# Gateloop and low-rank mixer: 96 packed rows, group 0's logarithms summed in the product, the sign from bits, and another written-out order

## The chip, the cores and the metric

The kernel runs on 1 core of one Trainium2 chip. The metric is the device time of one execution in microseconds; lower is better. A core has five engines that run side by side, each through its own list of instructions in order: TensorE (PE, with its weight loads PEld), VectorE (DVE), ScalarE (ACT), GpSimd (POOL) and SyncE (SP, which here only issues transfers). Semaphores tie them together.

## The reference, cut to what matters

```python
mag = np.sqrt(a_re * a_re + a_im * a_im)
scale = np.minimum(mag, 0.999) / (mag + 1e-06)
a_re_n, a_im_n = (a_re * scale, a_im * scale)
for t in range(S):
    ar, ai = (a_re_n[:, :, t, :, None], a_im_n[:, :, t, :, None])
    new_re = ar * S_re - ai * S_im
    new_im = ar * S_im + ai * S_re
    S_re, S_im = (new_re + kv, new_im)       # kv = outer(k_t, v_t)
    y[:, :, t] = q_t @ S_re
...
h = xt @ U @ V                               # xt: y's heads side by side, turned
u = x + h.transpose(0, 2, 1)
return u + np.maximum(u @ w_ch1, 0.0) @ w_ch2
```

Four batches, eight heads of 48, sequences of 768. The first half is a recurrence with a complex decay for each channel; the second mixes tokens with a product of rank 32 and channels with a layer of width 1536. All is in float32.

## The kernel before, in words

**Chunks and groups.** The recurrence is done in 24 chunks of 128 tokens, six to a batch, two to a group: groups 0 to 11. A decay is split into the logarithm of its magnitude and its angle, both are summed over tokens, and exponentials and sines of the sums weigh q and k, so that the recurrence becomes products of matrices. Then a mixer follows for every two chunks: 12 mixers.

**Gates of a group** (`gates`, `magnitudes_of` from line 637). DVE and ACT form the logarithm `l` of the magnitude and the tangent of half the angle. For group 0 (`SPREAD`) the work is split by chunk, and `l` is made of two parts: DVE takes the maximum (line 658) and adds `y` to it (line 660). PE sums `l` over tokens with one matmul for `es ps` and one for `ef ps` (line 696), and block totals `tot` (line 735). From group 3 on (`SPLIT`) `l` is split in two words first (lines 670 to 673), line 692 sums them and line 741 makes the totals. The sign of the real part comes from its bits on DVE in groups 0 to 2 (`BITS`, line 678), and from ACT's Sign in the others (line 681). There ACT also turns the angle into fractions of a turn and adds a quarter (line 763), after DVE's product in line 760. ACT loads another table between the exponentials and the sines (line 381).

**Preparation of a chunk** (`prep`). DVE weighs q and k by `es`, multiplies them with cosine and sine (`cs`) into `QKC`, and PE transposes `QKC` head by head (line 860), in two halves of 64 tokens side by side. A head's `QKC` has the real part in columns 0 to 47 and the imaginary part in 64 to 111, with zeros between, so transposed rows are 112 (`DQ`); the tables `T` of block decays have the same rows, with ones in between from POOL (line 469), and come from `E` by four transfers of SP (line 719). ACT copies the transposed halves to `QK` (line 871).

**A chunk's products** (`chain`). `inner` (lines 907, 910), `corners` (971), the state products `dk` (996) and the output `y` (1027, 1035), with scalings of `QK` on DVE between them and four transfers of SP that place diagonal blocks (`AT`).

**Mixers** (`mixer`). `rank` (1070), ACT's copy of it to `r` (1076), `mixed` (1089), then `up` (1122) and `down` (1313, 1356), or `few` (1222) in late mixers. Mixer 0 starts early, before its low-rank part is known, and is put right: `rT` (1136) transposes `r`, DVE copies it, `rw ps` (1145) multiplies it with the weights, ACT copies that, and `fix` (1161) is added to `h`. The weights come as float64 and are turned to float32 by DVE and ACT (line 384 for ACT, 573 to 580 for DVE).

**The order** is written out by hand. Every operation of every engine has a place in one long list; the table `ORDER` gives, for each engine and kind of work, the places of its operations. The instructions are issued in the order of places, so each engine's list is in that order; a place says nothing of a time. `SPARE` gives, for some places, how many units of filler PE issues ahead of the operation there: `idle` (line 1519) multiplies the identity with one to three copies of itself, 128 columns a unit, into a PSUM tile that the next product overwrites. A float32 matmul runs as two passes and is counted twice in the profile; a transposition is counted once. So the order fixes what each engine has to do ahead of any given operation. Ahead of ACT's copy of `r` stand 210 ACT operations, and ahead of `rT` 111 PE operations besides fillers; ahead of the first transposition of chunk 7 stand 271 ACT and 228 DVE operations.

Of the kernel before, what the change touches and what calls it, by code (L numbers as in the profile page):

```python
# [10 lines left out]
FP = mybir.dt.float32  # L11
# [28 lines left out]
        ("POOL", "load"): {0: [14], 1: [34], 1.5: [84], 2: [31]},  # L40
        ("DVE", "load"): {1: [58]},
# [6 lines left out]
        ("ACT", "gates"): {0: [1, 2, 4, 6, 7, 16, 17, 22, 23, 29, 28, 45, 70, 71], 1: [24, 27, 38, 39, 41, 42, 46, 47, 65, 64, 67, 68], 2: [129, 108,  # L48
# [10 lines left out]
        ("DVE", "gates"): {0: [5, 8, 13, 18, 19, 54, 49], 1: [30, 21, 40, 43, 44, 51, 50], 2: [111, 143, 156, 185, 169], 4: [277, 322, 323, 372, 356],  # L59
# [10 lines left out]
        ("ACT", "angles"): {0: [72, 86, 98, 100, 103], 1: [76, 106, 112, 114, 126], 2: [210, 231, 251, 240, 241, 242, 263, 269, 271], 4: [375, 395,  # L70
# [5 lines left out]
        ("DVE", "angles"): {0: [81, 89], 1: [87, 107], 2: [211, 232, 252], 4: [376, 402, 425], 6: [589, 597, 602, 612, 625, 626, 665], 8: [698, 716,  # L76
# [4 lines left out]
        ("DVE", "prep"): {0: [85, 104, 110], 1: [121, 128, 145], 2: [226, 250, 265], 3: [203, 304, 309], 4: [373, 424, 427], 5: [443, 470, 472], 6:  # L81
# [159 lines left out]
def kernel(  # L241
# [19 lines left out]

    nc = tc.nc
    B, H, S, D = q.shape
    DP = 64
    DQ = DP + D
    DM = H * D  # L270
    FF = moe_w_ch1.shape[1]
    R = moe_U.shape[1]
    KD = DM // 128
# [1315 lines left out]
```

## Time and profile before

| what | value |
|---|---|
| median of 3 runs | 629.38 us (629.16 to 630.21) |
| span of the profiled execution, first to last instruction | 627.0 us |
| PE busy | 609.9 us, of which fillers (line 1519) 30.6 us |
| DVE busy | 499.7 us |
| ACT busy | 415.8 us |
| transfers | 45.7 MB, mean 73 GB/s |

The median lies 2.4 us above the profiled span; no other time is given for the profiled execution itself. In the profile's lines an instruction group reads as line, engine, operation, result<-inputs, shape and count, then busy time and the mean of one in ns, then the idle time of its engine in front of it with what ended that. A line of a window reads as stretch, length, then busy time and count for each engine, the granted clock of TensorE, the share of time in which the DMA engines were busy, and GB/s. A line of the timeline starts with the start and the length in microseconds; there, "x6" are six instructions in a row.

### The profile page before, as it was taken

To read this page: it belongs to the slowest core of one execution; us is meant where nothing else is said; L and a number is where in the kernel's file an instruction comes from. 1 tells how busy PE (TensorE), PEld (TensorE's weight loads), DVE (VectorE), ACT (ScalarE), POOL (GpSimd) and SP (SyncE) were. 2 spreads that over 40 slices of the span, in tenths; PEclk is the share of its full clock that TensorE was granted. 3 is DMA by queue.
4 is the path that set the end of the run, shared out by engine and by line. 5 is a ranking of instruction groups with operands and counts; after the bars stand their busy time and mean duration, and the time that the engine had idled before them with its cause. 6 is when DMAs were issued, how large, how long until landed. Compare 5 with 4: busy or idle time off the path is not lost.

```text
span 627.0 us, 23447 instructions
## 1 busy us (share of the span) xinstructions
PE 609.9 (97%) x10380; PEld 526.2 (84%) x10380; DVE 499.7 (80%) x887; ACT 415.8 (66%) x807; POOL 38.1 (6%) x79
## 2 busy tenths in 40 slices
PE   6998989999999999999999999999999999999998
PEld 3566767666889889889989989888999998999997
DVE  6899999888999979758977867788989884464554
ACT  6999999999898988687787867688433431202010
POOL 5000000000001010010000100000100100000100
PEclk7999999999999999999999999999999999999999
DMA  8864565644143252541512512601203020000101
GB/s 211 191 146 115 135 136 132 155 111 104 33 80 76 50 120 44 99 89 28 99 37 46 113 40 46 124 19 25 63 21 60 9 51 3 1 1 1 45 14 44
DMA packets 173685, 45.74 MB, mean 73 GB/s; under 512 B 167632, under 2 KB 170384, under 8 KB 173584
## 3 DMA queue, kind: packets, MB, share of 16 engines
q1 hardware_dynamic: 171376, 39.90, 30.1%
q0 software_dynamic: 2208, 4.35, 2.1%
q8 instruction: 81, 1.33, 0.9%
q14 instruction: 20, 0.16, 0.1%
HBM read 33.59 MB, written 4.72 MB: 61 GB/s over the span
## 4 chain that ended last, share of the span: by engine, by line
PE 77%; ACT 4%; DVE 3%; DMA 1%; issue 1%; SPq 0%; ACTq 0%; DVEq 0%
PE down L1356 24%; PE up L1122 15%; PE few L1222 11%; PE dk L996 3%; PE tr L860 3%; PE y L1035 3%; PE inner L910 2%; PE down L1313 2%; PE inner L907 2%; PE tot L741 2%; PE y L1027 2%; PE mixed L1089 2%; PE es ps L692 1%; PE ef ps L692 1%; PE uTp L1107 1%; PE corners L971 1%
## 5 line engine op out<-in xcount | busy, mean ns | idle before, releaser
L1122 PE MATMUL up<-uT,w 128*128 128x256 f32 x504 | 116.9, 383 | 0.0
L387 DVE TENSOR_TENSOR QK<-QK,T 112x512 f32<-112x512 f32 (+2 forms) x144 | 102.1, 732 | 8.4 <-PE inner L910 4.3
L1122 PEld LDWEIGHTS up<-uT,w 128*128 128x128 f32 x504 | 93.6, 190 | 12.5
L1356 PE MATMUL down<-w,h 128*128 128x192 f32 x396 | 72.2, 331 | 0.0
L384 ACT ACTIVATE gate<-gate 128x768 f32<-128x768 f32 (+1 forms) x82 | 64.8, 795 | 7.4 <-DVE GS L791 3.2
L1356 PEld LDWEIGHTS down<-w,h 128*128 128x128 f32 x396 | 64.1, 190 | 1.5 <-issue 0.7
L871 ACT COPY QK<-tr 112x512 f32<-112x512 f32 x96 | 51.2, 590 | 14.6 <-PE tr L860 14.3
L390 DVE TENSOR_TENSOR xo<-down,xo 128x192 f32<-128x192 f32 (+1 forms) x79 | 29.9, 387 | 27.5 <-PE down L1356 27.0
L387 DVE TENSOR_TENSOR QKC<-qk,cs 128x768 f32<-128x768 f32 x44 | 41.7, 955 | 6.3 <-ACT cs L384 3.6
L1230 ACT COPY h<-few 128x512 f32<-128x512 f32 x30 | 17.2, 586 | 40.8 <-PE few L1222 40.8
L1356 PE MATMUL down<-stage 128*128 128x192 f32 x198 | 37.6, 331 | 0.0
L1111 ACT COPY uT<-uTp 128x384 f32<-128x384 f32 x22 | 10.0, 479 | 41.4 <-PE uTp L1107 26.9
L1222 PE MATMUL few<-gate,w 128*128 128x128 f32 x280 | 34.8, 275 | 0.0
L1298 POOL DMA_DIRECT2D out_dram<-xo x32 | 19.2, 644 | 243.3 <-DVE xo L390 140.0
L860 PEld LDWEIGHTS tr<-ident,QKC 64*112 64x112 f32 x768 | 24.5, 130 | 10.7 <-issue 4.7
L1222 PEld LDWEIGHTS few<-gate,w 128*128 128x128 f32 x280 | 33.3, 192 | 0.0
L1356 PEld LDWEIGHTS down<-stage 128*128 128x128 f32 x198 | 32.1, 190 | 0.7 <-issue 0.2
L779 POOL DMA_DIRECT2D gate<-F x15 | 12.0, 799 | 327.9 <-DVE w L578 113.5
L860 PE MATMUL tr<-ident,QKC 64*112 64x64 f32 x768 | 29.4, 221 | 2.3 <-DVE QKC L387 1.6
L381 ACT ACT_TABLE_LOAD x24 | 30.8, 1283 | 1.1 <-PEq L1573 0.7
L384 ACT ACTIVATE h<-up 128x512 f32<-128x512 f32 x42 | 24.6, 596 | 9.8 <-PE up L1122 9.5
L976 ACT COPY AT<-corners 32x128 f32<-32x128 f32 x96 | 24.2, 255 | 9.6 <-PE corners L971 8.3
(200 smaller groups left out, 1285.4 us busy)
## 6 DMA issues: line engine op xcount, KB each, us to landing
stage<-in_moe_w_ch_dram SPq DMA_DIRECT2D x12, 768.0 KB, 5.0
qk<-in_q_dram SPq DMA_DIRECT2D x24, 192.0 KB, 3.2
qk<-in_k_dram SPq DMA_DIRECT2D x24, 192.0 KB, 2.7
VP<-in_v_dram SPq DMA_DIRECT2D x24, 192.0 KB, 3.6
gate<-in_a_re_dram SPq DMA_DIRECT2D x22, 192.0 KB, 3.4
gate<-in_a_im_dram SPq DMA_DIRECT2D x22, 192.0 KB, 3.4
AT<-DG SPq DMA_DIRECT2D x96, 32.0 KB, 2.3
T<-E SPq DMA_DIRECT2D x48, 48.0 KB, 2.9
```

Of the source, the lines that this page charges most:

```text
L381: ACT(1.37, rank, lambda: nc.scalar.preload_act_table_set(name), writes=[TABLE])
L384: return nc.scalar.activation(out=o, in_=i, func=f, **kw)
L387: nc.vector.tensor_tensor(out=o, in0=a, in1=b, op=OP.mult)
L390: nc.vector.tensor_tensor(out=o, in0=a, in1=b, op=OP.add)
L860: nc.tensor.transpose(out=get(*ps[r])[0:DQ, h], in_=get(*qkc)[at, h].rearrange("p u d -> p (u d)")[:, 0:DQ], identity=ident[at, at], tile_ ...
L871: nc.scalar.copy(out=to, in_=a)
L976: ACT(0.36, RR, lambda r=r, u=u: nc.scalar.copy(out=get(*ATi).rearrange("p (a u) t -> p a u t", u=2)[r:r + BLK, :, u, BLK:2 * BLK], in_=ge ...
L996: nc.tensor.matmul(out=get(*dk[r])[x:end, h], lhsT=get(*ks)[at, h, x // DP, 0:end - x], rhs=get(*VPi)[at, h], start=True, stop=True, tile_ ...
L1122: nc.tensor.matmul(out=get(*ps)[:, e], lhsT=w1[:, f, (ff + e) * 128:(ff + e + 1) * 128], rhs=get(*uT)[:, f], start=(f == 0), stop=(f == KD ...
L1222: nc.tensor.matmul(out=get(*ps)[:, q], lhsT=w()[:, q * 128:(q + 1) * 128], rhs=v[0](), start=(n == 0 and q == 0), stop=True, skip_group_ch ...
L1298: queue.dma_start(out=out[b, c * CH:(c + 1) * CH, lo:hi], in_=get("xo", i)[:, lo:hi])
L1356: nc.tensor.matmul(out=get(*to)[:, part], lhsT=x(j), rhs=y[:, j], start=(first and j == 0), stop=(j == KH - 1), skip_group_check=not first)
```

## The change

1. **96 rows.** `DQ` is 96: a head's real and imaginary part stand side by side in `QKC`, `T` and `QK`, without columns between. POOL's memsets of `T` go, and those of `QKC` shrink to 16 columns at the end. The state products still take 64 and 48 columns of a head's `QKC`; the last 16 of these belong to the next head and their sums are not read.
2. **Group 0's logarithms** are no longer added on DVE. PE sums both parts: two products where there was one in `es ps`, `ef ps` and each block total of chunks 0 and 1.
3. **The sign from bits** in all groups, on DVE. ACT's Sign and its Identity in groups 3 to 11 go; the quarter is added by the operations that split the angle in two words.
4. **Another order.** All of `ORDER` and `SPARE` is new, from a search in which every transfer took a microsecond longer. The units of filler are 108 instead of 153: 39 ahead of the first `es ps` (before: 8), none behind place 606, which is `rT` (before: the last at 718; `rT` had 596). Ahead of ACT's copy of `r` stand 213 ACT operations, ahead of `rT` 112 PE operations besides fillers, and ahead of the first transposition of chunk 7 260 ACT and 221 DVE operations.

```diff
-SPARE = {20: 8, 32: 9, 62: 1, 66: 1, 73: 1, 82: 5, 91: 1, 113: 6, 116: 1, 119: 8, 140: 8, 153: 6, 157: 4, 167: 1, 168: 1, 207: 6, 216: 1, 217: 1, 282:
-         1, 352: 2, 436: 1, 514: 5, 518: 5, 527: 4, 546: 4, 547: 25, 551: 12, 596: 2, 601: 1, 606: 3, 624: 1, 632: 3, 646: 1, 653: 1, 664: 1, 672: 2,
-         678: 5, 694: 1, 695: 1, 717: 1, 718: 2}
+SPARE = {20: 39, 82: 6, 94: 2, 106: 10, 119: 5, 140: 9, 155: 3, 157: 2, 191: 6, 227: 6, 257: 6, 263: 2, 277: 3, 311: 3, 336: 2, 439: 2, 606: 2}
...
+    DQ = 2 * D
     DP = 64
-    DQ = DP + D
...
+    SUMMED = (0,)
...
-        QKC.append(singles.tile([128, H, 2, DP], FP, name="QKC%d" % n))
-        nc.gpsimd.memset(QKC[n][:, :, :, D:DP], 0.0)
+        QKC.append(singles.tile([128, H * DQ + DP - (DQ - DP)], FP, name="QKC%d" % n))
+        nc.gpsimd.memset(QKC[n][:, H * DQ:], 0.0)
...
         TS.append(singles.tile([DQ, GC, H * NTOT], FP, name="T%d" % n))
-        nc.gpsimd.memset(TS[n], 1.0)
...
-            if on_dve:
+            if g in SUMMED or g in SPREAD:
                 DVE(c_one(W), R1, lambda: nc.vector.tensor_scalar(out=t(l), in0=t(l), scalar1=-0.5, scalar2=-LNMAX, op0=OP.mult,
                                                                   op1=OP.max), [], [L])
-                DVE(cd, R1, lambda: add(t(l), t(l), t(y)), Y, [L])
+                if g not in SUMMED:
+                    DVE(cd, R1, lambda: add(t(l), t(l), t(y)), Y, [L])
...
-            if g in BITS:
-                DVE(c_one(W), R1, lambda: nc.vector.tensor_scalar(out=t(n).bitcast(U32), in0=t(ar).bitcast(U32), scalar1=0x80000000,
-                                                                  scalar2=INV_PI, op0=OP.bitwise_and, op1=OP.bitwise_or), AR, [N])
-            else:
-                ACT(ca + 0.09, R1, lambda: act(t(n), t(ar), AF.Sign, bias=tiny), AR, [N])
+            DVE(c_one(W), R1, lambda: nc.vector.tensor_scalar(out=t(n).bitcast(U32), in0=t(ar).bitcast(U32), scalar1=0x80000000,
+                                                              scalar2=INV_PI, op0=OP.bitwise_and, op1=OP.bitwise_or), AR, [N])
...
-                    PE(0.65, R1, lambda: nc.tensor.matmul(out=get(*to), lhsT=m.bitcast(FP), rhs=of(l, i), start=True, stop=True),
-                       [L, name], [to, ("sums", g, i)], takes=[keeps], steps=2)
+                    def each():
+                        for u, a in enumerate(parts):
+                            nc.tensor.matmul(out=get(*to), lhsT=m.bitcast(FP), rhs=of(a, i), start=(u == 0), stop=(u == len(parts) - 1))
+                    PE(0.65 * len(parts), R1, each, [L, name] + [y + (i,)] * (g in SUMMED), [to, ("sums", g, i)], takes=[keeps], steps=2 * len(parts))
...
-                        out=get(*tt)[u * DP:u * DP + D, 0:hi - lo, w * HH * NTOT:(w + 1) * HH * NTOT],
+                        out=get(*tt)[u * D:(u + 1) * D, 0:hi - lo, w * HH * NTOT:(w + 1) * HH * NTOT],
...
-            if g not in BITS:
-                ACT(ca + 0.09, R2, lambda: act(t(z), t(z), AF.Identity, scale=1.0 / math.pi, bias=fourth), [], Z)
...
-                    ACT(c_act(DM), R2, lambda: nc.scalar.copy(out=of(a, i), in_=of(z, i)), [zi], [a + (i,)])
+                    ACT(c_act(DM) + 0.09, R2, lambda: act(of(a, i), of(z, i), AF.Identity, bias=fourth), [zi], [a + (i,)])
...
-                        nc.tensor.transpose(out=get(*ps[r])[0:DQ, h], in_=get(*qkc)[at, h].rearrange("p u d -> p (u d)")[:, 0:DQ],
+                        nc.tensor.transpose(out=get(*ps[r])[0:DQ, h], in_=get(*qkc)[at, h * DQ:(h + 1) * DQ],
...
-                    for x, end in ((0, DP), (DP, DQ)):
-                        nc.tensor.matmul(out=get(*dk[r])[x:end, h], lhsT=get(*ks)[at, h, x // DP, 0:end - x], rhs=get(*VPi)[at, h],
+                    for x, w in ((0, DP), (DP, D)):
+                        nc.tensor.matmul(out=get(*dk[r])[x:x + w, h], lhsT=get(*ks)[at, h * DQ + x:h * DQ + x + w], rhs=get(*VPi)[at, h],
```

In the order's first places, for instance, the transfers are issued otherwise (the numbers are places; kinds 0 to 0.1 are group 0's real and imaginary parts and the prefix matrix, 1 and 2 the first two blocks of weights, 1.2 the masks, 1.3 and 1.4 chunk 0's q, k and v):

```diff
-        ("SP", "load"): {0.0: [0, 3, 2666, 2654, 2670], 0.05: [11, 12], 0.1: [9], 1: [10], 1.2: [57], 1.3: [15, 59], 1.4: [83], 2: [35], 2.5: [56,
+        ('SP', 'load'): {0.0: [0, 4, 2655, 2640, 2658], 0.05: [11, 7], 0.1: [9], 1: [22], 1.2: [21], 1.3: [55, 73], 1.4: [91], 2: [23], 2.5: [79, 83],
```

More of the change, by code (lines that the diff above doesn't have):

```diff
@@ L76 @@
-        ("DVE", "angles"): {0: [81, 89], 1: [87, 107], 2: [211, 232, 252], 4: [376, 402, 425], 6: [589, 597, 602, 612, 625, 626, 665], 8: [698, 716,
[4 rows of a table removed]
-        ("DVE", "prep"): {0: [85, 104, 110], 1: [121, 128, 145], 2: [226, 250, 265], 3: [203, 304, 309], 4: [373, 424, 427], 5: [443, 470, 472], 6:
[6 rows of a table removed]
-        ("ACT", "prep"): {0: [115, 117, 120, 122], 1: [158, 147, 154, 160], 2: [266, 270, 283, 281], 3: [319, 320, 327, 318], 4: [442, 439, 446, 445],
[4 rows of a table removed]
-        ("DVE", "rest"): {0: [118, 149, 155, 175, 159, 170, 194], 1: [174, 229, 234, 259, 209, 235, 248, 253], 2: [288, 315, 325, 366, 291, 314, 324,
[8 rows of a table removed]
@@ L102 @@
-        ("DVE", "levels"): {0: [123, 135, 148, 136, 137, 152], 1: [177, 192, 202, 195, 198, 225], 2: [292, 302, 308, 301, 303, 312], 3: [328, 371,
[9 rows of a table removed]
-        ("ACT", "levels"): {0: [138], 1: [215], 2: [305], 3: [378], 4: [468], 5: [530], 6: [766], 7: [839], 8: [947], 9: [1006], 10: [1152], 11:
[14 rows of a table removed]
-        ("ACT", "rest"): {0: [191, 182, 200, 201, 219, 223, 222], 1: [255, 261, 256, 258, 280, 279, 278], 2: [342, 341, 336, 335, 385, 390, 391], 3:
[10 rows of a table removed]
-        ("ACT", "small"): {0: [595, 285, 307, 492, 396, 554, 590, 549, 623, 636], 1: [744, 791, 777, 807, 782, 856, 859], 2: [984, 978, 1088, 1139,
[4 rows of a table removed]
@@ L172 @@
-        22: [2039, 2077]},
-        ("DVE", "mixing"): {7: [2018, 2019, 2021, 2030, 2032, 2024, 2040, 2102, 2108, 2115, 2120, 2125, 2027]},
-}
-SPARE = {20: 8, 32: 9, 62: 1, 66: 1, 73: 1, 82: 5, 91: 1, 113: 6, 116: 1, 119: 8, 140: 8, 153: 6, 157: 4, 167: 1, 168: 1, 207: 6, 216: 1, 217: 1, 282:
-         1, 352: 2, 436: 1, 514: 5, 518: 5, 527: 4, 546: 4, 547: 25, 551: 12, 596: 2, 601: 1, 606: 3, 624: 1, 632: 3, 646: 1, 653: 1, 664: 1, 672: 2,
-         678: 5, 694: 1, 695: 1, 717: 1, 718: 2}
[9 rows of a table added]
+        ('POOL', 'load'): {0: [10], 1: [62], 1.5: [578], 2: [42]},
@@ new lines @@
+        ('DVE', 'load'): {1: [26]},
[6 rows of a table added]
+        ('ACT', 'gates'): {0: [2, 3, 5, 13, 17, 14, 19, 46, 47, 33, 34, 44, 69, 70], 1: [15, 8, 25, 29, 28, 32, 40, 57, 52, 49, 59, 65], 2: [121, 61,
[10 rows of a table added]
+        ('DVE', 'gates'): {0: [6, 1, 27, 18, 63, 56], 1: [16, 12, 30, 31, 67, 39], 2: [90, 145, 153, 196, 148], 4: [221, 306, 319, 353, 327], 6: [441,
[10 rows of a table added]
+        ('ACT', 'angles'): {0: [71, 85, 93, 92, 99], 1: [81, 97, 102, 108, 114], 2: [211, 235, 249, 248, 246, 250, 255, 254, 269], 4: [364, 390, 411,
[5 rows of a table added]
+        ('DVE', 'angles'): {0: [76, 86], 1: [84, 98], 2: [214, 236, 253], 4: [371, 391, 416], 6: [554, 557, 563, 591, 611, 612, 624], 8: [699, 727,
[4 rows of a table added]
@@ new lines @@
+        ('DVE', 'prep'): {0: [88, 103, 107], 1: [110, 118, 131], 2: [208, 256, 262], 3: [239, 287, 309], 4: [398, 419, 424], 5: [429, 442, 490], 6:
[6 rows of a table added]
+        ('ACT', 'prep'): {0: [111, 115, 117, 116], 1: [127, 130, 156, 159], 2: [264, 270, 271, 272], 3: [316, 308, 335, 323], 4: [448, 444, 436, 437],
[4 rows of a table added]
+        ('DVE', 'rest'): {0: [113, 146, 158, 201, 144, 154, 167], 1: [198, 205, 222, 252, 228, 260, 265, 268], 2: [280, 321, 334, 351, 298, 333, 348,
[8 rows of a table added]
+        ('DVE', 'levels'): {0: [124, 135, 139, 133, 137, 147], 1: [160, 179, 195, 178, 186, 210], 2: [275, 289, 291, 290, 293, 312], 3: [350, 370,
[9 rows of a table added]
@@ new lines @@
+        ('ACT', 'levels'): {0: [138], 1: [189], 2: [303], 3: [386], 4: [488], 5: [541], 6: [743], 7: [839], 8: [933], 9: [1033], 10: [1170], 11:
[14 rows of a table added]
+        ('ACT', 'rest'): {0: [183, 204, 176, 200, 219, 225, 231], 1: [238, 258, 241, 243, 285, 286, 282], 2: [366, 384, 363, 376, 407, 405, 410], 3:
[10 rows of a table added]
+        ('ACT', 'small'): {0: [605, 296, 415, 467, 385, 526, 596, 610, 619, 622], 1: [733, 802, 778, 770, 812, 835, 749], 2: [919, 916, 1060, 1082,
[4 rows of a table added]
+        ('DVE', 'small'): {0: [278, 608, 627, 631, 637, 634, 671, 653, 645, 650, 750, 720], 1: [713, 719, 712, 825, 819, 842, 896, 921, 873, 901, 915,
[25 rows of a table added]
@@ new lines @@
+        ('POOL', 'small'): {0: [996, 823], 1: [1053, 1096, 1110], 2: [1389, 1184, 1397], 3: [1668, 1429, 1495], 4: [1716, 1633, 1738], 5: [2067, 1867,
+        1944], 6: [2229, 2076, 2183], 7: [2315, 2247, 2301], 8: [2639, 2477, 2533], 9: [2631, 2522, 2659], 10: [2610, 2600, 2625]},
+        ('POOL', 'angles'): {6: [598], 8: [725, 740], 10: [879, 906], 12: [1067], 14: [1255, 1292], 16: [1418, 1477], 18: [1648], 20: [1807, 1864],
+        22: [1994, 2031]},
+        ('DVE', 'mixing'): {7: [1995, 2009, 1996, 2047, 2060, 1983, 1985, 2091, 2106, 2116, 2108, 2115, 2095]},
+}
@@ L301 @@
     PL = H * HC
-    BITS = range(SPLIT[0])
     PUT = (0, 2), (4, 6), (8, 10)
@@ L443, in w2_of @@
         return w2.rearrange("p (j x) m -> p j x m", x=2)[:, :, x, y * DH:(y + 1) * DH]
-    leps, lmax, tiny = column("leps", math.log(1e-6)), column("lmax", LNMAX), column("tiny", 1e-30)
+    leps, lmax = column("leps", math.log(1e-6)), column("lmax", LNMAX)
     magic, fourth, quarter = column("magic", MAGIC), column("fourth", 0.25), column("quarter", math.pi / 2)
@@ L726, in of_blocks @@
             lo = first
-            ps, e = ("tot", i), ("E", g)
+            ps, e, parts = ("tot", i), ("E", g), (y, l) if g in SUMMED else (l,)
             psum(ps, "T", [128, HH, NTOT])
@@ L734, in sums @@
                         h, w = at + (u * HH + p) * D, 64 if u == 0 else D
-                        nc.tensor.matmul(out=get(*ps)[u * 64:u * 64 + w, p], lhsT=get(*l)[:, h:h + w], rhs=total, start=True,
-                                         stop=True, tile_position=(0, u * 64))
+                        for n, a in enumerate(parts):
+                            nc.tensor.matmul(out=get(*ps)[u * 64:u * 64 + w, p], lhsT=get(*a)[:, h:h + w], rhs=total, start=(n == 0),
+                                             stop=(n == len(parts) - 1), tile_position=(0, u * 64))
             def at_once():
@@ L744, in of_blocks @@
             else:
-                PE(0.51, R1, sums, [l, ("total", 0), ("sums", g)], [ps], way=1, takes=[e], steps=4 * HH)
+                PE(0.2 + 0.31 * len(parts), R1, sums, [l, ("total", 0), ("sums", g)] + [y + (i,)] * (g in SUMMED), [ps], way=1, takes=[e],
+                   steps=4 * HH * len(parts))
             used = 2 * D if g in SPLIT else 64 + D
@@ L833, in T_of, with turns_of_heads @@
         return get("T", g)[:, i - GROUPS[g][0]].rearrange("p (h b) -> p h b", h=H)[:, :, at:]
+    def turns_of_heads(qkc):
+        return get(*qkc)[:, 0:H * DQ].rearrange("p (h u d) -> p h u d", u=2, d=D)
     def prep(i):
@@ L988, in chain @@
         for r in parts_k:
-            psum(dk[r], "Y", [128, H, D], [128, H, DP])
+            psum(dk[r], "Y", [128, H, D], [128, H, HC])
         def state(h0):
```

24 lines of the change are left out of this document (8 added, 16 removed), and 246 rows, old and new, of the table ORDER.

## The prediction

> **What bounds the kernel now.** I read the page first, for the shares of the span, then busy time by stage, then the timeline at the stage's border, then the groups for single prices.
>
> ```profile
> span 627.0 us, 23447 instructions
> PE 609.9 (97%) x10380; PEld 526.2 (84%) x10380; DVE 499.7 (80%) x887; ACT 415.8 (66%) x807; POOL 38.1 (6%) x79
> PE   6998989999999999999999999999999999999998
> DVE  6899999888999979758977867788989884464554
> ACT  6999999999898988687787867688433431202010
> ```
>
> PE has 97% of the span, but not all of that is work: line 1519 issues filler matmuls whose result nobody reads. The next two answers split the span at two landmarks, the first `rT` matmul (line 1136, at 119.3 us) and the first transposition of chunk 7 (line 860, at 163.0 us): first all instructions, then the fillers alone.
>
> ```profile
> 0.00:119.30 119.30, 106.66 (x2222) 76.23 (x2222) 110.58 (x189) 109.06 (x212) 8.41 (x32) 0.97 0.64 153
> 119.30:163.00 43.70, 42.66 (x424) 28.18 (x424) 38.46 (x57) 39.23 (x61) 2.50 (x3) 1.00 0.41 98
> 163.00:627.00 464.00, 460.58 (x7744) 421.76 (x7734) 350.66 (x644) 267.54 (x536) 27.16 (x44) 1.00 0.24 50
> ...
> 0.00:119.30 119.30, 24.59 (x70) 14.10 (x70) 0.97 0.64 153
> 119.30:163.00 43.70, 6.01 (x22) 3.60 (x22) 1.00 0.41 98
> 163.00:627.00 464.00, 0.00 (x0) 0.00 (x0) 1.00 0.24 50
> ```
>
> The columns after the length are busy time and count of PE, PEld, DVE, ACT and POOL (in the filler rows PE and PEld alone), then clock, DMA share and GB/s. In the first stage PE's useful time is 106.66 − 24.59 = 82.1 us of 119.3, while DVE and ACT are busy for 110.6 and 109.1: these two set the pace. In the second, PE's useful time is 42.66 − 6.01 = 36.65, below ACT's 39.23 and DVE's 38.46: they still set it, just. From 163 us on there is no filler and PE idles 3.4 us, nearly all of it the tail behind the last matmul: from here the time is PE's work.
>
> So time can be won in three ways: reaching 119.3 sooner, having nothing to fill between the landmarks, or less PE work afterwards.
>
> **The change part by part.** *Up to the landmark `rT`.* It waits for ACT's copy of `r` (line 1076), and ACT works in the order written down.
>
> ```profile
> 118.34 0.70 PE L1519 MATMUL fix<-ident 128*128 128x256 f32 x2
> 118.82 0.47 ACT L1076 COPY r<-rank 128x384 f32<-128x384 f32 x1
> 119.34 0.85 PE L1136 MATMUL rT<-fold,r 64*128 64x32 f32 x6 [0.30 <-ACT r L1076]
> ...
> L384 ACT ACTIVATE gate<-gate 128x768 f32<-128x768 f32 x70 | 58.8, 843 | 4.7 <-DVE GS L791 3.2 <-DVE gate L390 0.9 <-DVE gate L387 0.3
> L384 ACT ACTIVATE h<-up 128x512 f32<-128x512 f32 x42 | 24.6, 596 | 9.8 <-PE up L1122 9.5
> L384 ACT ACTIVATE F<-ph,magic 128x384 f32<-128x384 f32 x24 | 13.9, 579 | 8.2 <-PE ph L796 7.4 <-PE ph L804 0.4 <-PE ph L801 0.3
> L384 ACT ACTIVATE stage<-stage 128x768 int32<-128x768 uint32 x10 | 9.1, 913 | 0.0
> L384 ACT ACTIVATE w<-stage 128x768 f32<-128x768 f32 x10 | 9.1, 916 | 0.0
> L384 ACT ACTIVATE gate<-gate,tiny 128x768 f32<-128x768 f32 x9 | 8.4, 938 | 0.0
> L384 ACT ACTIVATE gate<-gate,fourth 128x768 f32<-128x768 f32 x9 | 8.4, 931 | 2.3 <-DVE gate L760 2.1
> ```
>
> Counted in the two order tables, 210 ACT operations stand ahead of that copy before and 213 after. After has six that before has not: four conversions of `w2` (two of 916, two of 913 ns), one `F` (579) and a square of group 4 (843). Three are gone: an `h` (596), and group 3's Sign (938) and Identity (931), which the change abolishes. 5.08 − 2.47 = 2.6 us more. A cross-check on DVE: up to the last scaling that `y` of chunk 5 needs, 169 operations before and 174 after; at that stage's mean of 110.58/189 = 0.585 us, five are 2.9 us. **I take 2.6 us later**, `rT` at 121.9.
>
> *Edits hidden in that stage.* The doubled matmuls of group 0:
>
> ```profile
> 15.35 0.81 PE L696 MATMUL es ps<-GL,mid 128*128 128x384 f32 x2
> 17.69 1.09 PE L735 MATMUL tot<-total,GL 128*64 128x32 f32 x32 [0.66 <-ACT es L384]
> L390 DVE TENSOR_TENSOR GL<-GL,gate 128x384 f32<-128x384 f32 x2 | 1.1, 568 | 0.3 <-ACT gate L384 0.2
> L678 DVE TENSOR_SCALAR gate<-gate 128x768 uint32<-128x768 uint32 x1 | 0.6, 559 | 0.0
> ```
>
> Four more products of 0.81 us and once more 1.09 us of block totals are 4.3 us of PE; its 24.6 us of fillers and 12.6 us of idling there cover them; uncovered they would cost 4.3 us. They save DVE two additions (1.1 us), already in the counts. The sign from bits costs DVE 0.56 us in each of nine groups, 5.0 us in all, and spares ACT 9 × (0.938 + 0.931) = 16.8 us. Only group 3 lies ahead of `rT` and is counted; the rest falls where PE sets the pace: nothing. The quarter moves into operations that exist: nothing.
>
> *The first microseconds.* After has 39 units of filler (13 matmuls, 26 passes) ahead of the first `es ps`, before 8, and four passes behind them where before had two.
>
> ```profile
> 0.00:10.00 10.00, 4.79 (x8) 2.69 (x9) 5.30 (x19) 5.96 (x11) 7.23 (x30) 0.90 0.78 184
> 10.00:20.00 10.00, 9.34 (x54) 5.69 (x53) 8.31 (x19) 7.25 (x16) 1.17 (x3) 0.75 1.00 240
> ...
> 1.42 3.58 PE L1519 MATMUL tr<-ident 128*128 128x384 f32 x6 [1.42 <-POOL ident masks.py:199]
> 8.79 1.62 PE L696 MATMUL es ps<-GL,mid 128*128 128x384 f32 x2 [3.79 <-DVE GL L390]
> 10.21 4.05 PE L1519 MATMUL tr<-ident 128*128 128x384 f32 x6
> 19.13 1.28 ACT L381 ACT_TABLE_LOAD   x1
> 28.29 1.99 PE L1519 MATMUL up<-ident 128*128 128x384 f32 x6
> ```
>
> The granted clock is 0.75 on the mean of 10 to 20 us and 1.00 from then on. Six passes take 4.05 us at half clock (the row at 10.21) and 1.99 at full (28.29). From 1.42 on, 26 passes end at 10.0 if all are fast and at 19.0 if all are slow. Before, PE restarted at 8.79 and was still slow at 10.21; I take six slow microseconds at most, so an end between 11.5 and 13. `es ps` then starts some 3 us later than at 8.79, but runs its four passes in about 1.3 us where two took 1.62. Adding ACT's operations in the new order, the table load falls at about 20.0 instead of 19.13, with one square (0.84 us) done in front of it that came later before: even. The bounds are −0.6 and +5. [...]
>
> *Between the landmarks.* Behind `rT` after has no filler left. Up to chunk 7's first transposition its lists hold 260 − 213 = 47 ACT and 221 − 179 = 42 DVE operations, where the stage before had 61 and 57. At this stage's means (39.23/61 and 38.46/57) they need 30.2 and 28.3 us. PE's own useful 36.65 us, less one `up` that moves behind the landmark (2.7), leave 34: PE is last by 4 us. So the **6.0 us of fillers go**; the 1.0 us in which PE idled I leave in.
>
> *After that* the PE list holds the same products; 464 us stay. The transpositions read 96 columns instead of 112:
>
> ```profile
> L860 PEld LDWEIGHTS tr<-ident,QKC 64*112 64x112 f32 x768 | 24.5, 130 | 10.7 <-issue 4.7
> ...
> L996 PEld LDWEIGHTS dk<-VP,QKC 64*64 64x64 f32 x704 | 24.7, 134 | 5.3 <-issue 1.5 <-DVE QKC L387 1.1 <-ACT xo L1046 0.9
> L741 PEld LDWEIGHTS tot<-total,GL 128*96 128x96 f32 x144 | 14.2, 164 | 0.7
> ...
> 163.09 1.09 PE tr L860 x32
> ...
> L384 ACT ACTIVATE E<-tot 96x128 f32<-96x128 f32 x18 | 4.9, 274 | 4.4 <-PE tot L741 4.4
> L384 ACT ACTIVATE E<-tot 112x128 f32<-112x128 f32 x6 | 1.7, 282 | 0.7 <-PE tot L735 0.6
> ```
>
> A pair of them, one in each half of the rows, takes 1.09/16 = 68 ns; the loads of 64 columns in `dk` last no less (134 ns) than these of 112 (130). So columns don't set their pace: nothing. Other bound: (164 − 134)/32 = 0.94 ns a column, 15 ns a load, 7.5 for each of 768 as two run side by side: −5.8 us. [...]
>
> *Moves I cost at nothing:* DVE and ACT work on 96 rows for 112 (the same 128 elements a row take 274 ns on 96 rows and 282 on 112), POOL's memsets of `T` (done by 3.3 us, first use past 30), its cast of `prefix_r` (behind `total` in its own queue, first needed in group 3), the DMA into rows 48 up. SP's queue is reordered: one of four `T` transfers now stands behind the 768 KB of weight block 3.
>
> ```profile
> stage<-in_moe_w_ch_dram SPq DMA_DIRECT2D x12, 768.0 KB, 5.0
> T<-E SPq DMA_DIRECT2D x48, 48.0 KB, 2.9
> ```
>
> Block 3 waits for DVE's last reading of block 1, by the DVE list about 22.5 us; with 5.0 + 2.9 us at the worst `T` is there at 30.4, and the first scaling wants it at about 30.5. Each microsecond beyond would cost one.
>
> **The sum:** 627.0 + 2.6 − 6.0 = 623.6 us. The timed runs have a median of 629.38, 2.4 above the profiled span; so **626.0 us**.
>
> **Rivals.**
> 1. *The pace stays with ACT and DVE behind `rT`* (slower). The chain `rT`, DVE's copy, `rw ps`, ACT's copies, `fix` needs answers at every link, and PE would idle as long as it filled: 629.4 + 2.6 = 632.0. For it: DVE and ACT are only a few microseconds above PE before. Against: 47 and 42 operations for 61 and 57. It decides once waits of 3.4 us come together there.
> 2. *Late start.* The 26 passes run slow for longer, or `T` comes late: 2 to 5 us, 628 to 631. Against: PE never stops before `es ps` now, where it stood still for 3.79 us.
> 3. *The extra 2.6 us aren't on the path*, since ACT idles 10 us in the first stage: 623.4. For it: the transfers are asked for earlier.
> 4. *Columns count after all*: half to all of 5.8 us: 620.2 to 623.1.
> 5. *PE idles unseen where it filled*: fillers go, waits come, `rT` keeps its time: 629.4.
>
> **How the numbers follow.** Forecast 0.53, own range 624 to 628.5; rival 1 0.15, rival 2 0.12, rival 3 0.10, rival 4 0.06, rival 5 0.04. A measurement tells about 0.2% (1.3 us) from no change. Faster: nearly all of the forecast, rivals 3 and 4, a little of 2: 0.67. Slower: rival 1 and part of 2: 0.20. Same: 0.13. The range takes in rival 3's 623.4 and rival 1's 632.0, with a margin below: 622.0 to 632.0.
>
> **What would show it.** `rT` at 122 ± 2 us; no filler behind it; PE busy, with under 2 us idle, from there to the tail; a pair of transpositions still at 65 to 68 ns; nothing after chunk 7 changed beyond 1 us. Wrong would be PE idling 4 us or more behind `rT`, `rT` past 125, or a second stretch at half clock.

## The result: slower by 0.38%, and the profile after

The changed kernel takes 631.02 us (median of 20 runs, 629.26 to 634.55), the kernel before 628.73 (20 runs on the same chip); the ratio is 1.0038, with a 95% interval of 1.0026 to 1.0051. The forecast was 626.0, faster. The profiled execution of after has a span of 630.2 us, 3.2 more than that of before.

The page of after, top and second part (40 slices of 15.8 us; PEclk is the granted clock in tenths):

```profile
span 630.2 us, 23482 instructions
PE 618.8 (98%) x10406; PEld 530.8 (84%) x10406; DVE 501.4 (80%) x893; ACT 402.3 (64%) x789; POOL 35.6 (6%) x76
PE   9999999899999999999999999999999999999998
DVE  6799999888999879868778876977988977573644
ACT  5999999787897797886696776866541432212010
PEclk9999999699999999999999999999999999999999
```

ACT lost 13.5 us of busy time (the forecast had counted 16.8 for the sign), DVE gained 1.7, and PE is idle in fewer slices than before. New is the 6 in the clock row: a stretch at half clock in the eighth slice, about 110 to 126 us. In before the clock was low only in the first 15 us (0.50 from 8.10 to 14.93).

The stages of after, split at the same landmarks as before (first `rT` matmul, first transposition of chunk 7), show length, then busy time and count of PE, PEld, DVE, ACT and POOL, clock, DMA share, GB/s. Behind it the same stretches for the filler line alone (PE and PEld):

```profile
0.00:127.21 127.21, 120.50 (x2272) 83.19 (x2273) 112.95 (x192) 111.95 (x215) 6.67 (x30) 0.96 0.65 149
127.21:162.60 35.39, 34.93 (x391) 22.73 (x390) 30.95 (x46) 28.10 (x47) 2.11 (x3) 1.00 0.40 89
162.60:630.20 467.60, 463.32 (x7749) 424.89 (x7746) 357.55 (x655) 262.25 (x530) 26.78 (x43) 1.00 0.25 50
```

```profile
0.00:127.21 127.21, 30.08 (x78) 15.48 (x78) 0.96 0.65 149
127.21:162.60 35.39, 0.07 (x1) 0.00 (x0) 1.00 0.40 89
```

The second stage did what was forecast: no filler, 35.39 us for 43.70, PE busy in all but 0.46 of them; and since one `up` (12 matmuls, 2.7 us) is done behind chunk 7's first transposition now, the third has 467.60 for 464.00. The loss is in the first: `rT` comes at 127.21, 7.9 us later than before and 5.3 later than forecast. PE itself holds it up: it idles 6.7 us in this stage, where before had 12.6. The timeline of PE ahead of `rT` (start, length, operation; in brackets the idle time before it and what ended it):

```profile
115.56 0.25 PE L972 MATMUL corners<-QK 96*32 96x32 f32 x2
117.38 0.65 PE L972 MATMUL corners<-QK 96*32 96x32 f32 x30 [1.57 <-issue]
117.96 1.94 PE L997 MATMUL dk<-VP,QKC 64*64 64x48 f32 x32
```

Two of 32 equal matmuls run, then PE stands still for 1.57 us, and "issue" says that it waits for nothing that the profile shows. Behind it, `dk` takes 1.94 us for 32 matmuls; at full clock (below, without the hole) 1.10. In the clock records of both profiles every stretch that a change of the clock ends is a whole number of steps of 3.413 us (in after 32 at full clock from 7.33 us on, then 3 at half, then 148 at full; in before 1 and 2). Stages of that length show both (same columns as above):

```profile
109.73:113.15 3.42, 3.42 (x84) 2.26 (x82) 3.42 (x8) 3.38 (x7) 0.00 (x0) 1.00 0.76 199
113.15:116.56 3.41, 2.31 (x69) 1.97 (x67) 3.41 (x7) 2.83 (x6) 0.00 (x0) 1.00 0.97 218
116.56:119.97 3.41, 2.59 (x63) 2.43 (x62) 0.92 (x3) 1.84 (x5) 0.00 (x0) 0.50 0.62 120
119.97:123.39 3.42, 3.42 (x64) 2.89 (x66) 3.42 (x6) 2.38 (x5) 0.18 (x1) 0.50 0.59 99
123.39:126.80 3.41, 3.41 (x25) 1.32 (x22) 2.35 (x3) 1.96 (x5) 0.77 (x1) 0.50 0.21 26
```

In the window of the hole PE is busy for 2.31 us of 3.41, and from its end on the clock is 0.50 for three windows, 10.24 us. The matmuls there are small. For an estimate of their load I weigh each by its weights' share of the filler's 128*128, the largest in the kernel, and by 0.32 us per 384 elements (in after filler passes start 0.32 us apart from 7.35 us on, at full clock, and 0.64 apart ahead of that); by this the window comes to 24% of a stretch full of filler, here called 24% of the array. By the same estimate the lowest window of before behind 20 us, cut at the steps of its own clock record, comes to 41%, and none there is at half clock. So in after the window ahead of the half clock is one with PE 68% busy.

What the hole is, the transfers tell. The first answer is for 109 to 114.6 us, the second for 114.6 to 117.5 (packets, MB, share of 16 engines):

```profile
q1 hardware_dynamic: 2324, 1.17, 78.7%
```

```profile
q1 hardware_dynamic: 1928, 0.31, 65.2%
q8 instruction: 1, 0.02, 2.6%
```

The queue "q8 instruction" carries 82 packets of 16 KB (16,384 bytes each, 1.34 MB on the page) in the whole execution of after, and PE has 20,964 records (weight loads, matmuls, waits), about 256 for a packet. In before it is 81 packets for 20,922 records. I call 256 records a block, and a packet of this queue a fetch. None begins between 109 and 114.6, while a 768 KB weight block and two transfers of 192 KB are under way and the packets of q1 take 78.7%; one starts at 114.69, and 2.7 us later PE goes on. Now count PE's records up to a hole and take off 256 for every fetch that began before the last one: at all six holes of after that end in "issue" (36.5, 41.8, 65.1, 115.8, 184.7 and 452.9 us) 449 or 450 are left, 1.75 blocks of 256, so the holes lie whole blocks apart, and each ends 2.5 to 2.9 us after the last fetch began. My reading is that PE had used what it held at the start and what the earlier fetches brought, and waited for the next block; the profile itself names only "issue".

The theories, then. **Fetch and clock:** late fetches make holes, a hole among small matmuls drops the clock, and that delays `rT`. **Late start:** the 26 filler passes hold up `es ps`, and ACT's loss there reaches `rT`. **Pace:** ACT and DVE would bring `rT` that late anyway.

### The profile page after: what moved, and what is told of

Read it like the earlier page. It is cut to its first block, busy times and chain, and to the rows that moved or that the text cites. A ratio compares the mean times of both kernels' runs of the same rounds, so it can differ in the third digit from the quotient of the medians.

```text
span 630.2 us, 23482 instructions
## 1 busy us (share of the span) xinstructions
PE 618.8 (98%) x10406; PEld 530.8 (84%) x10406; DVE 501.4 (80%) x893; ACT 402.3 (64%) x789; POOL 35.6 (6%) x76
## 3 DMA queue, kind: packets, MB, share of 16 engines
q8 instruction: 82, 1.34, 1.0%
## 4 chain that ended last, share of the span: by engine, by line
PE 87%; ACT 9%; issue 1%; DVE 1%; DMA 1%; SPq 0%; POOL 0%; DVEq 0%; ACTq 0%; POOLq 0%
PE down L1357 24%; PE up L1123 16%; PE few L1223 11%; PE dk L997 3%; PE tr L861 3%; PE y L1036 3%; PE inner L911 3%; PE down L1314 3%; PE y L1028 2%; PE inner L908 2%; PE tr L1520 2%; ACT gate L382 2%; PE mixed L1090 2%; PE tot L739 2%; ACT L379 2%
## 5 line engine op out<-in xcount | busy, mean ns | idle before, releaser
L385 DVE TENSOR_TENSOR QK<-QK,T 96x512 f32<-96x512 f32 (+2 forms) x144 | 102.3, 725 | 12.8 <-PE inner L908 5.4
L1123 PEld LDWEIGHTS up<-uT,w 128*128 128x128 f32 x504 | 93.7, 190 | 12.6
L872 ACT COPY QK<-tr 96x512 f32<-96x512 f32 x96 | 50.9, 584 | 9.6 <-PE tr L861 9.0
L861 PEld LDWEIGHTS tr<-ident,QKC 64*96 64x96 f32 x768 | 23.6, 123 | 9.3 <-issue 3.8
L997 PEld LDWEIGHTS dk<-VP,QKC 64*64 64x64 f32 (+1 forms) x1408 | 26.0, 128 | 6.1 <-issue 3.0
L997 PE MATMUL dk<-VP,QKC 64*64 64x48 f32 (+1 forms) x1408 | 29.6, 219 | 1.1 <-ACT xo L1047 0.4
```

The source lines that it names most:

```text
L385: nc.vector.tensor_tensor(out=o, in0=a, in1=b, op=OP.mult)
L861: nc.tensor.transpose(out=get(*ps[r])[0:DQ, h], in_=get(*qkc)[at, h * DQ:(h + 1) * DQ], identity=ident[at, at], tile_position=(r * HC, 0))
L872: nc.scalar.copy(out=to, in_=a)
L997: nc.tensor.matmul(out=get(*dk[r])[x:x + w, h], lhsT=get(*ks)[at, h * DQ + x:h * DQ + x + w], rhs=get(*VPi)[at, h], start=True, stop=True, ...
L1123: nc.tensor.matmul(out=get(*ps)[:, e], lhsT=w1[:, f, (ff + e) * 128:(ff + e + 1) * 128], rhs=get(*uT)[:, f], start=(f == 0), stop=(f == KD ...
```

## The experiments

All ratios are to the kernel before on the same chip, with 95% intervals.

**Fillers against the half clock**, e1 being after with

```diff
-336: 2, 439: 2, 606: 2}
+336: 2, 439: 2, 560: 3, 566: 6, 606: 2}
```

and in e6 with `566: 3` alone in the filler table.

> After with 9 more units of filler (3 matmuls, 6 passes, some 1.9 us of PE) around the y products of chunk 4, where the array is least loaded ahead of the stretch at half clock. Clock theory (the half clock from 116.6 to 126.8 us is what delays rT): no stretch at half clock there, rT near 124 us instead of 127.2, span 627 to 628, ratio to before 0.998 to 1.000. Pace theory (ACT and DVE would bring rT that late with any clock): rT stays at 126 us or later, the 1.9 us of filler are added or hidden, ratio 1.003 to 1.006. Late-start theory: no change of the ratio, 1.004.

> After with only 3 units of filler (one matmul, two passes, 0.65 us) ahead of the corners of chunk 5. Clock theory: a window there has its load raised from 0.24 to about 0.4 of the array, so the half clock stays away in most runs; 1.3 us less filler than with 9 units: span 625.5 to 627, ratio 0.999 to 1.001. If 9 units worked because they gave the fetch time: part of the hole remains, half clock in some runs, ratio 1.001 to 1.004.

e1: 1.0020 (1.0009 to 1.0031). The clock row has no low slice, none of its 11 runs had a mean clock under 0.999, and `rT` is at 124.45 although 1.95 us of filler stand ahead of the corners. The clock row of its page, and its timeline:

```profile
PEclk9999999999999999999999999999999999999999
```

```profile
121.65 2.22 PE L1071 MATMUL rank<-xo,UV 128*32 128x384 f32 x16
124.45 0.85 PE L1137 MATMUL rT<-fold,r 64*128 64x32 f32 x6
```

`rank` takes 2.22 us for the 2.79 of after. The ratio lies between the ranges of the two theories; it is the clock and `rT` that decide. e6: 1.0018 (1.0000 to 1.0036), a mixture: six of 12 runs kept the clock, with a median span of 626.05 us, and the others lie between 627.8 and 629.6. In its profile (clock kept, span 625.4) `rT` is at 122.62, near the forecast's 121.9, although a hole of 0.63 us is left ahead of the corners. So pace falls: ACT and DVE do not bring `rT` later than that. Some of it is luck, though: in the profiles of e1 and e6 the clock came up at 4.5 us, in that of after at 7.3, and with the same fillers their first `es ps` starts 1.4 us earlier (11.43 and 11.40 for 12.83). The runs of after order themselves by the clock too. Their median spans are 627.55 us (two runs) at a mean clock of 0.997, 629.1 (11) at 0.995 and 630.2 (three) at 0.992, and the longest has 632.8 at 0.987. That is 1.1 to 1.6 us for each window of 3.4 us at half clock, holes that come with it included, and none of the 20 is without such a window.

**Two transfers later** (e5): a_re and a_im of chunk 8 are asked for behind the AT transfers of chunk 5.

```diff
-11: [528, 579, 558, 593, 760]
+11: [572.4, 579, 572.6, 593, 760]
```

> After, with two transfers of 192 KB (a_re and a_im of chunk 8) asked for behind the four AT transfers of chunk 5 instead of ahead of them; no filler added. Fetch theory (PE stands still for 1.57 us inside the corners of chunk 5 because the 16 KB of instructions it needs next were fetched late behind the data, and that hole lets the clock fall): the fetch near 114.7 us starts 1 us or more earlier, the hole is under 0.5 us, no half clock from 116 to 127 us in most runs, rT at 121 to 123, span 624 to 626, ratio 0.996 to 0.999. Load theory (the array's load is too low there even without the hole): hole gone but the half clock stays, ratio 1.002 to 1.004. If the fetch's delay has nothing to do with these transfers: hole and half clock as in after, 1.003 to 1.005.

1.0008 (0.9995 to 1.0021), without a filler. The fetch now starts by 113.5 us, and the hole is gone (timeline of PE):

```profile
115.85 0.62 PE L972 MATMUL corners<-QK 96*32 96x32 f32 x32
116.65 1.10 PE L997 MATMUL dk<-VP,QKC 64*64 64x48 f32 x32 [0.18 <-issue]
```

Six of 12 runs had no window at half clock, five had one and one had two. The fetch theory holds for the hole, but its forecast of the clock and of the ratio (0.996 to 0.999) was missed: in the profile one window is still at half clock, from 119.8 to 123.2 us, behind one that the estimate puts at 38% of the array, and `rT` is at 124.35 for the expected 121 to 123. So half clock can come there without the hole too, as the load theory had it.

**A shorter start** (e2: `20: 21` for `20: 39` in the filler table; e3: that and e1's fillers).

> After with 21 units of filler ahead of the first es ps where it has 39 (7 matmuls for 13). Late-start theory (ACT idles 3.36 us for es ps, and what it loses reaches rT): es ps starts at about 9 us, the table load moves from 20.5 to about 18 us, the half clock does not come back at 8 to 15 us, rT and the end come 2 to 3 us earlier, ratio 0.999 to 1.000. Clock theory: at 110 us PE is only 1.1 us behind before in work done, so the start gives 0 to 1 us, ratio 1.002 to 1.004, and the stretch at half clock ahead of rT stays.

> After with both edits of the two runs before: 9 units of filler around y of chunk 4, and 21 units for 39 at the start. Clock theory alone: as with the fillers alone, 627 to 628 us, ratio 0.998 to 1.000. Late-start theory alone: as with the short start alone, 0.999 to 1.000. Both at once, adding up: rT at 121 to 122 us, span 624 to 625, ratio 0.994 to 0.996, which is the forecast. Pace theory: no better than 1.003.

e2: 1.0094 (1.0061 to 1.0128); e3: 1.0078 (1.0052 to 1.0104). Every theory missed: both are slower than after. `es ps` started at 9.1 us and the table load at 16.85 for 20.53, as the late start has it; but the fetch ahead of the first `up` that waited started at 72.8, 2.6 us before PE went on at 75.37, and PE stood still (waits of PE in e2, 60 to 130 us: total, times, longest):

```profile
PE up L1123 <- issue: 2.0, 1, 2.0
PE corners L972 <- issue: 1.3, 1, 1.3
```

Each was followed by a stretch at half clock (3.4 us from 76.5, 6.8 from 117.4). Eight of its nine runs had three windows or more; the one with two had a span of 627.2 us. In e3's profile the same fetch is late too (a hole of 1.99 us at 73.6). So an earlier start is worth nothing while holes eat it.

**Before without its fillers at 108 to 112 us** (e4: `546: 4, 547: 25, 551: 12` taken out of the table of before).

> Before without the fillers ahead of three places near 108 to 112 us (41 units, some 8.8 us of PE at full clock, all in waiting time). Clock theory: the array's load falls under a third of a window there, a stretch at half clock of two or three windows appears between 108 and 122 us, rT comes 1 to 4 us later, ratio 1.001 to 1.006. If the fillers only fill waiting: the same time, ratio 0.999 to 1.001; if they stood in the way of real work: earlier, ratio 0.994 to 0.998.

1.0007 (0.9995 to 1.0018): the clock theory's expectation failed. No half clock appeared there, and the end did not move. `rT` came 1.6 us earlier (117.77), but that is not the fillers' doing: the table load, far ahead of them, came 1.5 us earlier already (17.63 for 19.13); the half clock behind 8 us lasted 3.4 us in this profile and 6.8 in that of before. In the order of before these fillers neither hold the clock nor cost anything.

**Parts alone, in the order of before:** the packing in 96 rows (e7: `DQ = 2 * D`, the packed tiles, `dk` and T rows that follow), and the sums of group 0 (e8: `SUMMED = (0,)`, the doubled matmuls, one DVE addition per chunk out of the order).

> Before with the packing of re and im rows in 96 alone; order, fillers, logarithms and signs as before. Forecast's step (the number of columns doesn't set the pace of the transpositions): ratio 0.999 to 1.001. Columns rival: 3 to 6 us less, ratio 0.990 to 0.995.

> Before with the sums of group 0 alone: logarithm and its bound summed by two matmuls each on PE, one DVE addition per chunk left out; rows, signs, order and fillers as before. Forecast's step (4.3 us of PE hidden in waiting and filler of the first stage): ratio 0.998 to 1.001, es ps not earlier than before by more than 0.6 us, table load within 1 us of 19.1 us or of where this chip has it. If PE's extra time is on the path: up to 4 us more, ratio 1.003 to 1.007.

e7: 0.9996 (0.9980 to 1.0012): the packing is worth nothing, as forecast. e8: 1.0067 (1.0047 to 1.0087), where "hidden" was forecast.

**Both cures, and the blocks shifted** (e9: the later transfers with e6's 3 units; e10: after with the fillers between 20 and 70 us as single units, 124 more instructions; e11: both).

```diff
+        step = 1 if 80 < at < 230 else AHEAD
         while run:
-            idle(min(run, AHEAD))
+            idle(min(run, step))
```

> After with both cures: the two transfers behind the AT transfers of chunk 5, and 3 units of filler ahead of its corners. Fetch and clock theory: no hole over 0.5 us between 100 and 127 us, clock 1.00 from there on in nearly all runs, rT at 121.5 to 123, span 625 to 626, ratio 0.998 to 1.000. If the two cures act on different losses and add up: 0.996 to 0.998. Pace theory (there is a floor set by ACT and DVE): no better than with the transfers alone, 1.0005 to 1.0015.

> After with the fillers between 20 and 70 us issued as single units (49 matmuls of 128 columns for 18 of up to 384): the same columns of filler, but 124 more instructions in PE's list ahead of 70 us, so every later block of 256 instructions ends 124 instructions earlier in the work. Transfers as in after. Fetch theory: the holes stay at the same place in a block (three quarters of a block past its start, counted in instructions) and so move in the work; the one at the corners of chunk 5 is gone, a hole over 1 us before rT in the profile is unlikely, ratio 0.999 to 1.002. If the hole belongs to that place in the work or to the transfers alone: hole of 1 us or more between 113 and 118 us and the half clock as in after, ratio 1.003 to 1.006.

> The two cures and the shifted blocks together. Fetch theory: holes left in the first 130 us under 0.5 us each; against the two cures alone up to 1 us less, ratio 0.996 to 0.9995, if the shift doesn't put another block's end into a dense stretch; in that case a hole there of 0.5 to 1.5 us shows in the trace and the ratio is 1.000 to 1.003.

e9: 1.0001 (0.9980 to 1.0021): eight of 12 runs at full clock, no hole over 0.3 us ending in "issue", `rT` at 123.57 with a start as late as after's (`es ps` at 12.92), 0.6 past the expected 121.5 to 123. The two cures together take `rT` from 127.21 to there. e10: 1.0107 (1.0075 to 1.0139), e11: 1.0112 (1.0082 to 1.0142), much slower, though the columns of filler are the same (fillers keep PE busy for 29.2 us in e10's profile and 30.2 in after's). The hole at the corners of chunk 5 did move, and it got worse (timeline of PE in e10):

```profile
98.50 0.22 PE L1036 MATMUL y<-G,QK 96*64 96x48 f32 x1
101.91 1.09 PE L1036 MATMUL y<-G,QK 96*64 96x48 f32 x15 [3.19 <-issue]
```

By the same count 1.76 blocks were used there too, and the fetch began at 99.1. So the holes of after and e10 go with a count of instructions and the moment of a fetch, not with a place in the work: that part of the expectation held, the hope that the new places are harmless did not.

**The start on top of the cures** (e12: e9 with `20: 30`; e15: with `20: 24`).

> The two cures with 30 units of filler ahead of the first es ps for 39 (10 matmuls for 13). Late-start theory: es ps starts 2 us earlier, near 10 to 11 us, the table load near 18.5, and the end comes 0.7 to 1.5 us earlier than with the cures alone. Fetch theory: 36 instructions fewer ahead shift the blocks, and transfers come at other moments: es ps and table load earlier, but holes at other places can eat it; the ratio lies between 0.997 and 1.004, and the trace tells by its holes which.

> The two cures with 24 units of filler at the start (8 matmuls) where the run before had 30. Start theory: es ps near 9.1 us, only 0.4 us earlier, since GL is ready no sooner: ratio 0.996 to 0.998, as with 30 units. Holes theory: 12 instructions fewer shift the blocks' ends by six matmuls; new holes can cost 0 to 3 us: 0.997 to 1.003.

e12: **0.9978 (0.9962 to 0.9994), faster than both kernels**, 626.65 us. Its start and its stages:

```profile
1.42 8.30 PE L1520 MATMUL tr<-ident 128*128 128x384 f32 x20 [1.42 <-POOL ident masks.py:199]
9.56 0.81 PE L693 MATMUL es ps<-gate,mid 128*128 128x384 f32 x2
```

```profile
0.00:120.46 120.46, 114.96 (x2269) 79.28 (x2269) 112.06 (x192) 111.96 (x215) 6.68 (x30) 1.00 0.69 156
120.46:156.42 35.96, 34.88 (x390) 22.69 (x390) 31.89 (x47) 28.19 (x47) 2.11 (x3) 1.00 0.41 93
156.42:624.10 467.68, 463.50 (x7754) 424.89 (x7746) 357.55 (x655) 262.26 (x530) 26.76 (x43) 1.00 0.25 50
```

`rT` is at 120.46, 3.1 us earlier than in e9. Some 1.5 us of that is the moment at which the clock came up (with the same fillers at the start, `es ps` is at 11.40 in e6 and at 12.92 in e9). Against e6, whose clock came up as early as e12's, it is 2.2 us, and e6 has the hole of 0.63. The median time is 1.6 us below e9's on the same chip. So the late start is true, once the holes are out. e15: 1.0035 (1.0009 to 1.0061), with two filler matmuls fewer (8 instructions with both passes and their loads; the expectation's 12 is a miscount, and so are the 36 of e12, which has 12 fewer than e9). Waits of PE in e15:

```profile
PE dk L997 <- issue: 3.3, 2, 2.5
PE inner L911 <- issue: 2.2, 2, 1.7
```

Its two runs without half clock had spans of 623.9 and 626.7 us, the others 628.5 to 633.9. So 8 instructions go with a difference of 0.57%. The two ran on different chips, each against before on the same chip.

**The sums again** (e13: e8 unchanged; e14: e8 with `20: 20` for `20: 8`, so that the clock is up before the first sum).

> Before with the sums of group 0 alone, a second look at the same kernel. If the loss is holes at the ends of blocks of 256 instructions: again ratio 1.005 to 1.008, with holes or a half clock behind 163 us that together make 2 us or more, at the same places in PE's list. If it is the price of the doubled matmuls at the start: rT and the first transposition of chunk 7 some 3 to 4 us later than with the packing alone (119.6 and 163.2 us), and nothing lost behind them.

> The sums alone, with 20 units of filler ahead of the first es ps for 8, so that PE never stands still before it and the clock is up when the doubled matmuls run. Start theory: table load 1.5 to 3 us earlier than with the sums alone (21.0 us), the end as much earlier, ratio 1.000 to 1.003. Holes theory: the start moves as much, but by 16 more instructions and other moments of the transfers the holes stay or move: ratio anywhere from 1.000 to 1.008, and holes of over 2 us in the trace if it stays above 1.004.

e13: 1.0054 (1.0037 to 1.0070); e14: 1.0022 (1.0003 to 1.0041), with the table load at 18.32 for 19.78. The third stage (chunk 7's first transposition to the end) of e7, e13 and e14, one row from each:

```profile
163.23:626.60 463.37, 459.97 (x7741) 421.26 (x7734) 350.33 (x644) 267.23 (x536) 27.15 (x44) 1.00 0.24 50
```

```profile
164.06:629.90 465.84, 461.05 (x7741) 422.03 (x7734) 350.56 (x644) 267.55 (x536) 27.14 (x44) 1.00 0.24 50
```

```profile
162.13:627.70 465.57, 460.67 (x7742) 421.80 (x7734) 350.77 (x644) 267.56 (x536) 27.14 (x44) 1.00 0.24 50
```

Of the 3.3 us that e13's profile has over e7's, 0.8 arise ahead of chunk 7, and the filled start of e14 takes away 1.9. The other 2.2 to 2.5 arise behind it, in work that nobody changed: about 1.4 of them are a wait for an AT transfer (0.9 to 1.0 us at 395) and holes in "issue" (0.35 and under). Why that transfer comes late was not found, so what the doubled matmuls cost beyond the start stays open. Nor was the order of before run with the 20 units alone: its start, at half clock from 8.1 to 14.9 us, may gain by them as well, and then the 0.2% of e14 is less than the sums cost.

## Why the prediction was wrong

- **`rT` 2.6 us later: the step that failed.** It came 7.9 us later. Missing was PE. The working took PE as covered ahead of `rT`, since in before it filled and idled there for 37 us; after has no filler between 93 and 126 us, so a hole of 1.57 us and 10.24 us at half clock fell on the path. In e9, without both and with as late a start, `rT` is at 123.57: 3.6 of the 5.3 us beyond the forecast are these two. The other 1.7 are about what the late start below costs. The count of ACT and DVE operations fits: from the table load to `rT` it is 100.2 us in before and 103.0 in e9, 2.8 more for the counted 2.6. But PE idles only 5.3 us ahead of `rT` in e9 too, so that ACT and DVE set this pace is not shown.
- **"A second stretch at half clock" stood in the list of what would be wrong, but was no rival with a price.** Rival 2's 628 to 631 ends where the result is, but its late start made only part of it.
- **The 6.0 us of fillers go: right.** 35.39 us for 43.70 between the landmarks, or 36.0 in e12; 2.7 of the difference are the `up` that moved behind. PE idled 0.46 us there; rival 1 and rival 5 fall. From `rT` to the end, though, after gains 4.7 us on before and e12 4.1, not 6.0.
- **"After that 464 us stay": off by 0.9 us** beyond that `up`. In after two holes (0.33 and 0.13) and two waits (0.51 and 0.18) make 1.15 of it.
- **First microseconds "even": not even.** The fillers ended at 12.99, inside the 11.5 to 13 of the forecast, but ACT idled 3.36 us for `es ps`, and the table load came at 20.53, for the forecast's 20.0 and 19.13 in before. With 20 passes for 26 (e12 against e9: 0.9978 and 1.0001) the end comes some 1.4 us earlier.

```profile
14.32 0.87 ACT L382 ACTIVATE es<-es ps 128x384 f32<-128x384 f32 x2 [3.36 <-PE es ps L693]
20.53 1.28 ACT L379 ACT_TABLE_LOAD   x1
```

- **Columns: right.** The packing alone gives 0.9996; a load lasts 123 ns for 96 columns (group in the page of after: busy, mean) and 130 for 112, and 32 transpositions still take 1.09 us to the next matmul. Rival 4 falls. The loads are 7 ns shorter, where the forecast's other bound had 15.

```profile
L861 PEld LDWEIGHTS tr<-ident,QKC 64*96 64x96 f32 x768 | 23.6, 123 | 9.3 <-issue 3.8
```

- **Doubled matmuls hidden: in part.** In the order of before they cost 0.5 to 0.7%; with more fillers at the start, 0.2% is left. Sign from bits: ACT's busy time fell by 13.5 us; it was not tried alone, so that nothing came of it, as forecast, is not shown.
- **Rival 3** (the 2.6 us aren't on the path) is not borne out: from the table load to `rT` it is 100.2 us in before, but 103.0 in e9 and 103.2 in e12, where the clock is up, and 106.7 in after.

Best version and forecast: e12 is at 0.9978, the forecast at 626.0/629.38 = 0.9946. Of the 2 us between them e12's profile shows a hole of 0.84 at 405.7 us and a wait of 0.73 at 125.0; the rest was not traced further. That e12 comes so near has luck in it: its `rT` is 1.4 us earlier than forecast, and behind it 1.9 of the 6.0 us are missing.

## What to carry to other kernels

Where PE sets the pace with small matmuls, look for idle time that ends in "issue" and for the packet of the instruction queue ahead of it: here 256 records were used up in 2.3 us (`corners`, `tot` and `inner` in e2, from 70.6 us), and PE went on 2.2 to 3.4 us after a late fetch began. Fillers that seem to fill only waiting may do more: with e1's nine units the half clock ahead of `rT` was gone in all 11 runs, while in e4 nothing was lost without the ones taken out (1.0007). So before removing them estimate the load of each clock step (3.41 us here) without them. And 8 instructions went with 0.57% between e12 and e15: a difference under 1% between two orders is not yet the merit of either.

## What the runs showed of the hardware

- The instruction queue q8 carried one packet of 16 KB for about 256 of PE's records (82 for 20,964 in after, 81 for 20,922 in before). Of the 70 holes in "issue" of over 0.1 us behind 30 us, in one profile each of both kernels and all 15 experiments, 68 lie at 1.75 to 1.76 blocks by the count above, and end 2.2 to 3.4 us after the late fetch began; the other two, of 0.17 us (e14) and 0.18 us (e5), do not. Behind 200 us the middle half of after's fetches begin at 0.7 to 1.0 blocks, 200 to 270 records short of the 1.75 at which the holes lie, and none before 0.6; the one ahead of the corners in after began at 1.54, some 55 short. The longest of these holes was 3.19 us (e10).
- In after the clock went from 1.00 to 0.50 at 116.56 us, behind a window with an estimated 24% of the array and PE 68% busy. It was still at 0.50 behind the window from 119.97, with PE busy throughout and 38% of the array, and back at 1.00 behind the next, at 43% (126.80). All its changes in the records of after and before lie whole steps of 3.413 us apart. The estimate gives no sharp threshold: in all profiles, behind 20 us, the clock fell after ten windows, at 12 to 38% (38% in e5, with PE 87% busy), while windows down to 28% (in e15, PE 63% busy) kept it, and at half clock it came back behind windows of 32 to 38% in e15, e11 and e5.
- The moment at which the clock comes up differs from run to run: in after it was 7.33 us (filler passes 0.64 us apart before, 0.32 after), in e1 4.51 with the same start, and `es ps` came at 12.83 and 11.43. So landmarks of two profiles can differ by 1.4 us from the start on.
